# Attention states, soft mixture and gated MLP in one kernel: the products with the states of the middle chunk are moved to the other two quarters of the array and next to a state link of the following iteration

## The chip, the cores and the metric

The kernel runs on one core of a Trainium2 chip. The metric is the device time of one execution in microseconds (us), as the median of the runs. Differences of under 0.5% (2 us) cannot be told from no change here.

## The reference

Everything is float32. A gated linear attention comes first, then a soft mixture of experts over all its tokens, then a gated MLP.

```python
# B, H, S, D = 4, 8, 768, 48
for t in range(S):
    state = alpha[:, :, t, :, None] * state + k[:, :, t] (x) v[:, :, t]    # D x D per head
    y[:, :, t] = q[:, :, t] @ state
x = y as 3072 tokens x 384
logits = x @ phi                         # 32 slots
d = softmax of logits over the tokens;  slot_input = d.T @ x
slot_out[e] = relu(slot_input[e] @ w1[e]) @ w2[e]      # 8 experts, 384 -> 1024 -> 384
x = softmax(logits over the slots) @ slot_out
out = (silu(x @ w_gate) * (x @ w_val)) @ w_out         # 384 -> 1536 -> 384
```

The last three weights come as 64-bit floats. The kernel loads them as pairs of 32-bit words and turns them into float32 itself.

## The kernel before

**Stages.** The attention takes the first 158 us. Then come the experts (first layer at L853, second at L910, until 193 us), and then the MLP with its output until the end. The MLP works with weights and activations split into two rounded parts (L1006, L1007, L1045).

**The attention.** A unit is one batch with two heads, so there are 16 units. The two heads lie on partitions 0 to 47 and 64 to 111. A unit has six chunks of 128 tokens and is worked in two halves of three chunks, so the loop of `fast()` has 32 iterations `g`, with `h = g % 2` the half. An iteration mixes steps of three halves, and the order of each engine's queue is the order in which the code is written (the schedule is manual). In the order of the queues, iteration `g` does this:

- `scan_w(g + 3)`, `scan_p(g + 3)` on DVE: running products of alpha (L307, L314), with small operations between (L306, L309, L310); `scale(g + 2)` on POOL (L325) multiplies q and k with them.
- `emit_st(g, 1 - h)`, the first link of the state chain: two small matmuls add the last state (L402), and ACT scales the sum and writes it to SBUF (L404).
- `emit_s(g + 1)`: the scores of the next half, six matmuls in pairs of 64 rows (L353), head 0 into one PSUM bank and head 1 into another (the tiles `s`).
- `emit_st(g, 2 - h)`, the second link; `emit_kt(g + 1)`, transposes of k (L371, copied by ACT at L374); `emit_xt(g - 1)`, transposes of the output (L462, L466); `emit_masks(g + 1)`: DVE masks the scores of head 0 into SBUF (L360), ACT copies those of head 1 (L362) and POOL masks them (L363); `emit_l(g - 1)`, the logits (L453).
- at the end of every fourth unit, steps of the mixture (`slot_steps`: `peak`, `exps`, `keep`, `e_tok`, `part`, `l_tok`, `c_norm`), one or a few to an iteration.
- `emit_past(g)`: the products of q with the states, two heads x three chunks (L420, the first chunk of a unit has none); `emit_dh(g + 1)`: what the chunks add to the state (L390); `emit_ip(g)`: the products of the masked scores with v, added to the same PSUM tile `y` (L432), which ACT copies whole into the tile `xt` (L434).

**The conversion.** Each of the 24 pieces of the gate and value weights is turned into float32 by four steps: `conv_y` on ACT (L249, writes a buffer `y` in the tile `near`), and `conv(0)`, `conv(1)`, `conv(2)` on DVE (L253, L257, L261); `conv(1)` and `conv(2)` read what `conv_y` wrote. Before, `conv_y` stands at the end of an iteration and the other three in the next one. They run in iterations 2 to 10, 13 to 18, 21 to 26 and 29 to 31.

**Loads.** SP issues all of them in the order of the code. `pump_units` loads the halves' inputs into buffers as these come free, `pump_gv` the weights to be converted, and `pump` the weights of the experts (`w1`, `w2`, 768 KB each) and of the output (`wo`), paced by a credit of `RATE` words an iteration. The last four `w2` go where `w1` blocks of the last group lay, so they wait for that group's matmuls (L853).

Of the kernel before, what the change touches and what calls it, by code (L numbers as in the profile page):

```python
# [33 lines left out]
LAST = 4  # L34
GV0, RATE = 1, 840
TINY = 2.0 ** -55
NEAR, ROUND = 31600, 19184
LA = 3
# [54 lines left out]
def attention_slots_mlp(ctx: ExitStack, tc: tile.TileContext, kq, at, vt, phi, w1, w2, wgv, wo, cst, out):  # L93
# [12 lines left out]
    negm = cs[:, 288:289]  # L106
    phs = const.tile([112, NU, NSL], F32, name="phs")
    tots = const.tile([112, B * NU, NC], F32, name="tots")
# [32 lines left out]
    def program(general):  # L141
# [15 lines left out]

        zn = {nm: [0] * n for nm, n in (("a", 4), ("p", 5), ("v", 4), ("w", 2), ("x", 2))}
        zsize = {"a": HW, "p": HB, "v": 288, "w": HW, "x": 384}
        for z in "a0 a1 p2 a2 p3 v0 w0 a3 p4 v1 w1 p0 v2 p1 v3 x0 x1".split():  # L160
            zn[z[0]][int(z[1])] = ar.alloc(zsize[z[0]], 1)
# [107 lines left out]
        NG = 24  # L269
        gvb, gvy, gvd = {}, {}, [0]  # L270

# [3 lines left out]
        def conv_y():  # L275
            i = gvd[0]
            if i < NG and ("wgv", divmod(i, 4)) in have:
                gvy[i] = to_f32_y(view(have["wgv", divmod(i, 4)]))

        def conv(part):  # L280
            i = gvd[0]
            if i not in gvy:
                return
            n, p = divmod(i, 4)
            raw = view(have["wgv", (n, p)])
            if n not in gvb:
                gvb[n] = need(BLK)
            dst = view((gvb[n][0] + GP * p, GP))
            if part == 0:
                to_f32_z(dst, raw)  # L290
            elif part == 1:
                to_f32_p(dst, gvy[i])
            else:
                to_f32_s(dst, gvy.pop(i))
                gvd[0] += 1
                r = have.pop(("wgv", (n, p)))
                z_g.append(r[0])
# [47 lines left out]
        def emit_s(g, c):  # L345
            n, h = sgs[g]
            k, q = view(kp[g]), view(qp[g])
            if c == 0:
                sps[g] = [pss(), pss()]
            t0 = c * CH  # L350
            o = c * CH
            for s in range(2):
                nc.tensor.matmul(sps[g][s][:, o:o + CH], lhsT=k[64 * s:64 * s + 64, t0:t0 + CH], rhs=q[64 * s:64 * s + 64, t0:t0 + CH], start=True, stop=True)  # L353
# [53 lines left out]

        yps = {}


        def emit_past(g):
            n, h = sgs[g]
            q = view(qp[g], 112)
            yps[g] = ps_y.tile([128, 512], F32, tag="y", name="y")
            for c in range(3):
                cc = 3 * h + c
                o = slice(c * CH, (c + 1) * CH)
                for s in range(2) if cc else ():
                    p = slice(0, 64) if s == 0 else slice(64, 112)
                    nc.tensor.matmul(yps[g][p, o], lhsT=gst[n, cc][p, 0:p.stop - p.start], rhs=q[p, o], start=(cc == max(1, 3 * h)), stop=False, skip_group_check=True)  # L420
            del qp[g]
            release(pair.pop(g), z_p, g + 5)

        def emit_ip(g):
            n, h = sgs[g]
            v = view(vv[g]).rearrange("p (c e) -> p c e", e=96)
            ps = yps[g]
            for c in range(3):
                o = slice(c * CH, (c + 1) * CH)
                for s in range(2):  # L430
                    p = slice(0, 64) if s == 0 else slice(64, 112)
                    nc.tensor.matmul(ps[p, o], lhsT=v[:, c, 48 * s:48 * s + p.stop - p.start], rhs=smk[g, s][:, c], start=False, stop=True, skip_group_check=True)  # L432
            xt[g] = (z_x.pop(0), 384)
            nc.scalar.copy(view(xt[g], 112), ps[0:112, 0:384])  # L434
            del smk[g, 0], smk[g, 1], yps[g]
            release(vv.pop(g), z_v, g + 4)

# [7 lines left out]
        def emit_l(g):  # L445
            n, h = sgs[g]
            b, u = units[n]
            if u == 0 and h == 0:
                lps[b] = ps_l.tile([128, 512], F32, tag="l", name="l")
            x = view(xt[g], 112)  # L450
            for j in range(3):
                t0 = j * CH
                nc.tensor.matmul(lps[b][32 * j:32 * j + 32, CH * h:CH * h + CH], lhsT=phs[:, u, :], rhs=x[:, t0:t0 + CH], start=(u == 0 and h == 0), stop=(u == NU - 1), skip_group_check=True)  # L453

# [13 lines left out]
        def slot_steps(b):  # L468
# [27 lines left out]
            def e_tok():  # L496
# [4 lines left out]
                nc.vector.tensor_copy(st["et"].rearrange("p r e -> p (r e)"), ps[:, 0:192])  # L501

            def part(between=lambda: None):
                ps = psm()
                o = NU * b % 5
                pieces = [(0, o, min(NU, 5 - o))] + [(5 - o, 0, NU - 5 + o)] * (o > 1)
                for r in range(2):
                    if r:
                        between()
                    for u, p, w in pieces:  # L510
                        for j in range(3):
                            nc.tensor.matmul(ps[32 * j:32 * j + 32, 96 * u:96 * u + 96 * w], lhsT=st["et"][:, r, 32 * j:32 * j + 32], rhs=xtok[:, p:p + w, 3 * r + j, :], start=(r == 0 and u == 0), stop=(r == 1), skip_group_check=True)
                if own:
# [62 lines left out]

        def fast():
            pump_units(4)

# [42 lines left out]
            for g in range(NSG):  # L622
                n, h = sgs[g]
                nxt = g + 1 < NSG
                if g + 3 < NSG:
                    scan_w(g + 3, lambda: conv(0))
# [22 lines left out]
                if g:  # L649
                    emit_l(g - 1)  # L650
                    release(xt.pop(g - 1), z_x, g + 1)
                    p = sgs[g - 1][0]
# [35 lines left out]
        def slow():  # L688
# [60 lines left out]
            while gvd[0] < NG:  # L749
                pump_gv()  # L750
                conv_y()
                for i in range(3):
# [376 lines left out]
def _arrays(q, k, v, alpha, moe_phi, moe_w1, moe_w2, moe2_w_gate, moe2_w_val, moe2_w_out):  # L1129
# [16 lines left out]
    vt = c(v.reshape(B, NU, 2, NC, CH, D).transpose(0, 1, 4, 3, 2, 5)).reshape(B, NU, CH, NC * 96)  # L1146
    ph = np.zeros((112, NU, NSL), np.float32)
    pr = moe_phi.reshape(NU, 2, D, NSL)
    for s in range(2):
        ph[64 * s:64 * s + 48] = pr[:, s].transpose(1, 0, 2)  # L1150
    w1 = c(moe_w1.reshape(NE, 3, 128, 2, 512).transpose(0, 3, 2, 1, 4)).reshape(NE, 2, 128, BLK)
# [30 lines left out]
```

## Time and profile before

| | |
|---|---|
| median of three runs | 394.04 us (393.09 to 395.3) |
| profiled execution | 395.87 us, its span 394.1 us |
| granted TensorE clock | 0.986 |
| PE busy | 372.6 us (95% of the span) |
| DVE busy | 291.0 us (74%) |
| ACT busy | 201.5 us (51%) |
| POOL busy | 103.9 us (26%) |

Busy shares are averages over stages with different limits. In the rows of the profile PE is TensorE's matmuls, PEld its weight loads, DVE VectorE, ACT ScalarE, POOL GpSimd and SP the queue that issues loads. Each float32 matmul shows as two records, so six matmuls stand as x12. A matmul's record is longer than the time in which it holds the array: records overlap, and the starts tell how fast they follow each other.

### The profile page before, as it was taken

What the parts mean: (1) busy time and instruction counts of PE and PEld (TensorE: products, weight loads), DVE (VectorE), ACT (ScalarE), POOL (GpSimd) and SP (SyncE); (2) the same over time, 40 slices, a digit from 0 to 9 for tenths busy, and PEclk for the clock granted to TensorE, in tenths of its full rate; (3) what the DMA queues carried; (4) which work ended last, traced back from release to release, by engine and by line L of the source; (5) the groups of instructions that cost most, each with busy time, mean ns of one, the idle gap of its engine ahead of it and who ended that gap; (6) DMA issues with size and microseconds to landing.
All of it is one profiled execution on the core that took longest, in us unless ns stands there. A gap on an engine that the chain in (4) does not pass through costs nothing.

```text
span 394.1 us, 8610 instructions
## 1 busy us (share of the span) xinstructions
PE 372.6 (95%) x3309; PEld 278.1 (71%) x3309; DVE 291.0 (74%) x566; ACT 201.5 (51%) x468; POOL 103.9 (26%) x105
## 2 busy tenths in 40 slices
PE   6999999998998998999799999999999999999992
PEld 3677767776776776434358868888888888888781
DVE  6999997997999773214598995767767877877550
ACT  1456665656466455423267655446445445446431
POOL 3378675788588741020300000000000000000000
PEclk8999999999999999999899999999999999999997
DMA  8899997999799849799900004104114114112002
GB/s 277 316 320 360 351 360 276 312 346 321 258 362 351 289 157 350 288 335 407 400 33 0 1 2 150 39 34 150 35 37 151 37 35 148 39 35 81 2 1 89
DMA packets 28627, 74.25 MB, mean 188 GB/s; under 512 B 3216, under 2 KB 11648, under 8 KB 28576
## 3 DMA queue, kind: packets, MB, share of 16 engines
q1 hardware_dynamic: 28256, 73.27, 52.3%
q8 instruction: 28, 0.46, 0.5%
q10 hardware_dynamic: 272, 0.21, 0.2%
q14 instruction: 23, 0.19, 0.1%
q0 software_dynamic: 48, 0.13, 0.1%
HBM read 68.87 MB, written 4.72 MB: 187 GB/s over the span
## 4 chain that ended last, share of the span: by engine, by line
PE 55%; DVE 6%; DMA 3%; ACT 3%; issue 2%; SPq 0%; DVEq 0%; ACTq 0%
PE m L1045 21%; PE acc L1045 11%; PE s L1006 4%; PE s L1007 4%; DMA near<-w 3%; PE s L853 3%; PE y L432 2%; PE y L420 2%; DVE near L1012 1%; DVE rnd L1020 1%; ACT near L249 1%; PE sw L975 1%; PE l L453 1%; PE m L402 1%; PE m L390 1%
## 5 line engine op out<-in xcount | busy, mean ns | idle before, releaser
L1045 PE MATMUL m<-rnd 128*128 128x512 f32 x432 | 129.2, 389 | 0.0
L1045 PEld LDWEIGHTS m<-rnd 128*128 128x128 f32 x432 | 81.1, 188 | 16.8
L1009 ACT ACTIVATE near<-s 128x512 f32<-128x512 f32 x72 | 43.1, 599 | 79.0 <-PE s L1006 77.3
L1045 PE MATMUL acc<-rnd 128*128 128x512 f32 x216 | 81.1, 392 | 0.8 <-DVE rnd L901 0.8
L325 POOL TENSOR_TENSOR far<-far 112x384 f32<-112x384 f32 x61 | 78.5, 1306 | 6.5 <-DVE tots L309 3.6
L1012 DVE TENSOR_TENSOR near<-near,s 128x512 f32<-128x512 f32 x72 | 49.4, 686 | 36.1 <-ACT near L1009 35.9
L1020 DVE TENSOR_TENSOR rnd<-near,rnd 128x512 fp32r<-128x512 f32 x72 | 49.4, 686 | 3.2 <-ACT rnd L1018 3.1
L1045 PEld LDWEIGHTS acc<-rnd 128*128 128x128 f32 x216 | 40.5, 188 | 10.3 <-DVE rnd L901 1.6
L1018 ACT CAST rnd<-near 128x512 fp32r<-128x512 f32 x72 | 44.3, 615 | 0.2 <-DVE near L1012 0.2
L404 ACT ACTIVATE far<-m,tots 112x48 f32<-112x48 f32 x80 | 24.1, 301 | 29.1 <-PE m L402 17.3
L307 DVE TENSOR_TENSOR_SCAN far<-far,r 112x388 f32<-112x388 f32 x32 | 30.8, 962 | 5.2 <-DMA far<-at 2.5
L353 PE MATMUL s<-far 64*128 64x128 f32 x384 | 30.6, 292 | 2.5 <-DVE r L306 2.1
L1116 DVE TENSOR_REDUCE amm<-near 112x1 f32<-112x768 f32 x32 | 30.3, 947 | 2.5 <-DMA near<-at 2.5
L363 POOL TENSOR_SCALAR_AFFINE_SELECT far<-far 128x384 f32<-128x384 f32 x32 | 19.1, 596 | 48.8 <-ACT far L362 48.8
L314 DVE TENSOR_TENSOR_SCAN far<-far,r 112x387 f32<-112x387 f32 x32 | 30.7, 959 | 1.1
L257 DVE SCALAR_TENSOR_TENSOR near<-near 128x384 uint32<-128x384 uint32 x36 | 24.2, 672 | 7.9 <-ACT near L249 7.0
L434 ACT COPY far<-y 112x384 f32<-112x384 f32 x32 | 15.3, 480 | 28.1 <-PE y L432 28.1
L432 PE MATMUL y<-far 128*48 128x128 f32 (+1 forms) x384 | 28.6, 274 | 0.0
L1006 PE MATMUL s<-rnd 128*128 128x512 f32 x72 | 28.3, 393 | 0.0
L1007 PE MATMUL s<-rnd 128*128 128x512 f32 x72 | 28.1, 391 | 0.0
L353 PEld LDWEIGHTS s<-far 64*128 64x128 f32 x384 | 24.4, 189 | 4.7 <-POOL far L325 2.6
L402 PE MATMUL m<-far,cs 64*64 64x48 f32 (+1 forms) x256 | 19.9, 229 | 6.5 <-ACT far L404 3.8
(163 smaller groups left out, 495.0 us busy)
## 6 DMA issues: line engine op xcount, KB each, us to landing
near<-w SPq DMA_DIRECT2D x18, 768.0 KB, 6.8
far<-kq SPq DMA_DIRECT2D x32, 384.0 KB, 4.8
far<-w SPq DMA_DIRECT2D x14, 768.0 KB, 6.7
near<-wgv SPq DMA_DIRECT2D x24, 384.0 KB, 5.4
far<-at SPq DMA_DIRECT2D x32, 194.0 KB, 4.7
near<-at SPq DMA_DIRECT2D x16, 339.1 KB, 3.3
far<-vt SPq DMA_DIRECT2D x32, 144.0 KB, 4.0
near<-wo SPq DMA_DIRECT2D x12, 384.0 KB, 8.7
```

The costliest lines, as they stand in the source:

```text
L307: nc.vector.tensor_tensor_scan(w[:, ::-1], a[:, ::-1], rst[:, ::-1], 0.0, ALU.mult, ALU.add)
L314: nc.vector.tensor_tensor_scan(a, a, rst[:, 0:387], 0.0, ALU.mult, ALU.add)
L325: eng.tensor_tensor(out=xv, in0=xv, in1=sv, op=ALU.mult)
L353: nc.tensor.matmul(sps[g][s][:, o:o + CH], lhsT=k[64 * s:64 * s + 64, t0:t0 + CH], rhs=q[64 * s:64 * s + 64, t0:t0 + CH], start=True, stop ...
L432: nc.tensor.matmul(ps[p, o], lhsT=v[:, c, 48 * s:48 * s + p.stop - p.start], rhs=smk[g, s][:, c], start=False, stop=True, skip_group_check ...
L1006: nc.tensor.matmul(pg, lhsT=swk[n][:, 128 * o:128 * o + 128], rhs=ctT[t % 4], start=True, stop=True)
L1007: nc.tensor.matmul(pv, lhsT=swk[n][:, 256 + 128 * o:256 + 128 * o + 128], rhs=ctT[t % 4], start=True, stop=True)
L1009: nc.scalar.activation(sg, pg, AF.Silu)
L1012: nc.vector.tensor_tensor(out=h_, in0=sg, in1=pv, op=ALU.mult)
L1018: nc.scalar.copy(hi, h_)
L1020: nc.vector.tensor_tensor(out=lo, in0=h_, in1=hi, op=ALU.subtract)
L1045: nc.tensor.matmul(p, lhsT=passes[j][0][:, sl], rhs=passes[j][1], start=(f == 0 and j == 0), stop=(f == NF - 1 and j == 2))
```

## The change

Five things are changed at once.

1. The middle chunk's products (`emit_past` and `emit_ip`, c = 1) write the other head's half of the output partitions (`swap`), so head 0's products with a state use rows 0 to 63 and columns 64 to 111 of the array and head 1's use rows 64 to 111 and columns 0 to 63. They no longer lie in the tile `y`, but in columns 384 to 511 of the bank that holds head 0's scores. The two score banks are now the same two tiles throughout (`sbank`). ACT copies the output in two instructions. The logits' weights `phi` and the pooled products (`x_rows`) undo the swap.
2. `emit_ip(g)` comes first and opens the accumulation; `emit_past(g)` and the copies follow in iteration `g + 1`, right behind the first state link and ahead of the scores.
3. `conv_y` and `conv(1)` stand behind `emit_kt`, in the same iteration as `conv(0)` and `conv(2)`. They run in iterations 1 to 10, 13 to 18, 21 to 26, 29 and 30.
4. When no inputs of halves are left to load, `pump` is no longer paced.
5. `xt` has one buffer in place of two, `phs` is doubled.

```diff
+        def swap(c):
+            return int(c == 1 and not general)
+        def y_out(g, s, c):
+            p = half(s ^ swap(c))
+            return sbank[0][p, 384:512] if c == 1 else yps[g][p, c * CH:(c + 1) * CH]
+        def emit_ip(g):
+            yps[g] = ps_y.tile([128, 512], F32, tag="y", name="y")
...
+                    o = y_out(g, s, c)
+                    e = 96 * c + 48 * s
+                    nc.tensor.matmul(o, lhsT=v[:, e:e + o.shape[0]], rhs=smk[g, s][:, c], start=(c < 2), stop=True, skip_group_check=True)
...
         def emit_past(g):
...
+                    o = y_out(g, s, c)
+                    nc.tensor.matmul(o, lhsT=gst[n, cc][half(s), 0:o.shape[0]], rhs=q[half(s), c * CH:(c + 1) * CH], start=False, stop=True, skip_group_check=True)
+            xt[g] = (z_x.pop(0), 384)
+            x = view(xt[g], 112)
+            nc.scalar.copy(x[:, CH:2 * CH], sbank[0][0:112, 384:512])
+            x, y = (r.rearrange("p (c t) -> p c t", t=CH)[:, 0::2] for r in (x, yps.pop(g)[0:112, 0:384]))
+            nc.scalar.copy(x, y)
...
+                now[0] = (0 < g <= 8 or g % 8 not in (3, 4)) and gvd[0] < NG and ("wgv", divmod(gvd[0], 4)) in have
+                emit_st(g, 1 - h)
+                if g:
+                    emit_past(g - 1)
...
-                conv(1)
-
-                emit_st(g, 1 - h)
                 if nxt:
                     for c in range(3):
                         emit_s(g + 1, c)
                 emit_st(g, 2 - h)
                 if nxt:
                     emit_kt(g + 1)
+                conv_y()
+                conv(1)
                 if g:
                     emit_xt(g - 1)
...
-                emit_past(g)
...
-                if GV0 <= g and (g < 8 or g % 8 not in (2, 3)):
-                    conv_y()
...
-                credit[0] = min(credit[0] + RATE, 2 * BLK)
+                credit[0] = min(credit[0] + RATE, 2 * BLK) if uloads else NEAR
...
+            emit_past(NSG - 1)
```

In the rows below, `s` are the score banks, `y` the output tile, `m` the PSUM tiles for small products, and `far` and `near` the two SBUF areas. What an instruction waits for stands in brackets, by the engine or DMA queue.

PE, in the products of an iteration's masked scores with v, before:

```order
L432 MATMUL y<-far 64x128
L432 MATMUL y<-far 48x128 [waits Pool_49]
L432 MATMUL y<-far 64x128
L432 MATMUL y<-far 48x128
L432 MATMUL y<-far 64x128
L432 MATMUL y<-far 48x128
```

and now:

```order
L429 MATMUL y<-far 64x128
L429 MATMUL y<-far 48x128 [waits Pool_49]
L429 MATMUL s<-far 48x128 [waits DVE_49]
L429 MATMUL s<-far 64x128
L429 MATMUL y<-far 64x128
L429 MATMUL y<-far 48x128
```

The middle pair writes the score bank. Its wait is for the DVE instruction L359 that masks the next half's scores out of that bank, in the same iteration.

PE, from the first state link to the second, before:

```order
L402 MATMUL m<-far,cs 64x48 [waits Activation_49]
L402 MATMUL m<-far,cs 48x48
L353 MATMUL s<-far 128x128 [waits DMAHW7_49,DVE_49,Pool_49]
L353 MATMUL s<-far 128x128 x5
L402 MATMUL m<-far,cs 64x48 [waits Activation_49]
```

and now:

```order
L401 MATMUL m<-far,cs 64x48 [waits Activation_49]
L401 MATMUL m<-far,cs 48x48
L440 MATMUL y<-far 64x128
L440 MATMUL y<-far 48x128
L440 MATMUL s<-far 48x128
L440 MATMUL s<-far 64x128
L440 MATMUL y<-far 64x128
L440 MATMUL y<-far 48x128
L352 MATMUL s<-far 128x128 [waits DMAHW7_49,Activation_49,Pool_49]
L352 MATMUL s<-far 128x128 x5
L401 MATMUL m<-far,cs 64x48
```

The products with the states now stand between the link and the scores, and the scores' wait for ACT is for the copy L443, which takes those products out of the score bank just ahead of them.

ACT, one iteration with a conversion, before:

```order
L434 COPY far<-y 112x384 [waits PE_49]
L249 ACTIVATE near<-near 128x384 [waits DMAHW7_49,DVE_49,Activation_49]
L404 ACTIVATE far<-m,tots 112x48 [waits PE_49] x2
L374 COPY far<-m 128x224 [waits PE_49,Activation_49]
L466 COPY far<-m 128x288 [waits PE_49]
L362 COPY far<-s 128x384 [waits Pool_49]
```

and now:

```order
L443 COPY far<-s 112x128 [waits DVE_49,PE_49,Activation_49]
L445 COPY far<-y 112x2x128 [waits PE_49,Activation_49]
L403 ACTIVATE far<-m,tots 112x48 [waits PE_49]
L373 COPY far<-m 128x336 [waits PE_49,Activation_49]
L249 ACTIVATE near<-near 128x384 [waits DMAHW4_49,DVE_49,Activation_49]
L477 COPY far<-m 128x288 [waits PE_49]
L361 COPY far<-s 128x384 [waits Pool_49]
```

The conversion's step L249 moved from ahead of the two links to behind the copy of the transposed k. On DVE the order of the operations is the same as before: L257, which reads what L249 writes, stands ahead of the mask.

More of the change, by code (lines that the diff above doesn't have):

```diff
@@ L34 @@
 LAST = 4
-GV0, RATE = 1, 840
+RATE = 840
 TINY = 2.0 ** -55
-NEAR, ROUND = 31600, 19184
+NEAR, ROUND = 31600, 19056
 LA = 3
@@ L269, in program @@
         NG = 24
-        gvb, gvy, gvd = {}, {}, [0]
+        gvb, gvy, gvd, now = {}, {}, [0], [False]
         def gv_part(n, k):
@@ L276, in conv_y @@
             i = gvd[0]
-            if i < NG and ("wgv", divmod(i, 4)) in have:
+            if now[0]:
                 gvy[i] = to_f32_y(view(have["wgv", divmod(i, 4)]))
@@ L281, in conv @@
             i = gvd[0]
-            if i not in gvy:
+            if not now[0]:
                 return
@@ L347, in emit_s @@
             k, q = view(kp[g]), view(qp[g])
[L348 to L349 removed]
+            sps[g] = sbank
             t0 = c * CH
@@ L406, in emit_st, with half @@
                 del dps[g]
-        yps = {}
+        yps, sbank = {}, []
+        def swap(c):
+            return int(c == 1 and not general)
+        def half(s):
+            return slice(0, 64) if s == 0 else slice(64, 112)
+        def y_out(g, s, c):
[3 more added lines that the diff above has]
+            yps[g] = ps_y.tile([128, 512], F32, tag="y", name="y")
+            v = view(vv[g])
+            for c in range(3):
+                for s in range(2):
+                    o = y_out(g, s, c)
+                    e = 96 * c + 48 * s
+                    nc.tensor.matmul(o, lhsT=v[:, e:e + o.shape[0]], rhs=smk[g, s][:, c], start=(c < 2), stop=True, skip_group_check=True)
+            del smk[g, 0], smk[g, 1]
+            release(vv.pop(g), z_v, g + 4)
         def emit_past(g):
@@ L452, in emit_l @@
                 t0 = j * CH
-                nc.tensor.matmul(lps[b][32 * j:32 * j + 32, CH * h:CH * h + CH], lhsT=phs[:, u, :], rhs=x[:, t0:t0 + CH], start=(u == 0 and h == 0), stop=(u == NU - 1), skip_group_check=True)
+                nc.tensor.matmul(lps[b][32 * j:32 * j + 32, CH * h:CH * h + CH], lhsT=phs[:, swap(j), u, :], rhs=x[:, t0:t0 + CH], start=(u == 0 and h == 0), stop=(u == NU - 1), skip_group_check=True)
         def emit_xt(g, between=lambda: None):
@@ L501, in e_tok, with x_rows @@
                 nc.vector.tensor_copy(st["et"].rearrange("p r e -> p (r e)"), ps[:, 0:192])
+            def x_rows(p, w, r, j):
+                x = xtok[:, p:p + w, 3 * r + j, :]
+                if swap(j):
+                    x = bass.AP(x.tensor, x.offset + 48, [list(x.ap[0]), list(x.ap[1]), [-48, 2], [1, 48]])
+                return x
             def part(between=lambda: None):
@@ L511, in part @@
                         for j in range(3):
-                            nc.tensor.matmul(ps[32 * j:32 * j + 32, 96 * u:96 * u + 96 * w], lhsT=st["et"][:, r, 32 * j:32 * j + 32], rhs=xtok[:, p:p + w, 3 * r + j, :], start=(r == 0 and u == 0), stop=(r == 1), skip_group_check=True)
+                            nc.tensor.matmul(ps[32 * j:32 * j + 32, 96 * u:96 * u + 96 * w], lhsT=st["et"][:, r, 32 * j:32 * j + 32], rhs=x_rows(p, w, r, j), start=(r == 0 and u == 0), stop=(r == 1), skip_group_check=True)
                 if own:
@@ L577, in fast @@
         def fast():
+            sbank.extend(pss() for _ in range(2))
             pump_units(4)
@@ L750, in slow @@
                 pump_gv()
+                now[0] = True
                 conv_y()
@@ L1146, in _arrays @@
     vt = c(v.reshape(B, NU, 2, NC, CH, D).transpose(0, 1, 4, 3, 2, 5)).reshape(B, NU, CH, NC * 96)
-    ph = np.zeros((112, NU, NSL), np.float32)
+    ph = np.zeros((112, 2, NU, NSL), np.float32)
     pr = moe_phi.reshape(NU, 2, D, NSL)
     for s in range(2):
-        ph[64 * s:64 * s + 48] = pr[:, s].transpose(1, 0, 2)
+        for x in range(2):
+            ph[64 * s:64 * s + 48, x] = pr[:, s ^ x].transpose(1, 0, 2)
     w1 = c(moe_w1.reshape(NE, 3, 128, 2, 512).transpose(0, 3, 2, 1, 4)).reshape(NE, 2, 128, BLK)
```

25 lines of the change are left out of this document (4 added, 21 removed).

## The prediction

> **What bounds the kernel now.** I read the page first, then the busy time by stretch of the span, then one iteration of the attention engine by engine, the waits, and the end of the experts.
>
> ```profile
> PE 372.6 (95%) x3309; PEld 278.1 (71%) x3309; DVE 291.0 (74%) x566; ACT 201.5 (51%) x468; POOL 103.9 (26%) x105
> ...
> DVE  6999997997999773214598995767767877877550
> ```
>
> PE is busy almost throughout. DVE's slices show nines in the attention (the first 16 of 40), so there a second engine is nearly full. The stretches below are cut at first links; after the stretch come its length and the busy time of PE, PEld, DVE, ACT and POOL, the granted clock, the DMA share and GB/s.
>
> ```profile
> 12.82:16.12 3.30, 3.30 (x52) 2.58 (x51) 3.06 (x7) 1.33 (x4) 0.65 (x2) 1.00 0.93 364
> 16.12:51.29 35.17, 33.90 (x511) 26.07 (x509) 33.67 (x74) 20.88 (x59) 23.91 (x25) 1.00 0.95 329
> 51.29:70.94 19.65, 18.69 (x273) 13.85 (x271) 16.44 (x38) 11.35 (x34) 12.44 (x13) 1.00 0.90 316
> 70.94:88.36 17.42, 16.90 (x256) 12.97 (x254) 16.72 (x39) 10.65 (x30) 13.76 (x13) 1.00 0.94 330
> ...
> 108.21:125.64 17.43, 16.91 (x257) 12.98 (x255) 16.73 (x39) 10.66 (x30) 13.78 (x13) 1.00 0.98 358
> ...
> 145.48:154.18 8.70, 8.45 (x130) 6.49 (x128) 3.75 (x8) 5.31 (x15) 2.51 (x4) 1.00 0.77 289
> ...
> 180.00:200.00 20.00, 17.52 (x175) 7.52 (x167) 12.72 (x25) 7.18 (x15) 3.53 (x3) 0.91 0.92 364
> ```
>
> The first row is iteration 0, the second iterations 1 to 8, then 9 to 12, 13 to 16, 21 to 24, and 29 and 30. In 1 to 8, 13 to 16 and 21 to 24 PE is 96 or 97% busy and DVE 96%: a wait on a chain over PE, ACT and DVE has no slack to hide in. Iterations 1 to 8, 13 to 16, 21 to 24, 29 and 30 are the 18 with a conversion and no large step of the mixture; they take 35.17 + 17.42 + 17.43 + 8.70 = 78.72 us, 4.37 each.
>
> Iteration 5, from one first link to the next, on PE, ACT and DVE:
>
> ```profile
> 33.55 0.38 PE L432 MATMUL y<-far 128*64 128x128 f32 x3
> 33.86 0.31 PE L402 MATMUL m<-far,cs 64*64 64x48 f32 x4
> 34.10 0.94 PE L353 MATMUL s<-far 64*128 64x128 f32 x12
> 35.17 0.31 PE L402 MATMUL m<-far,cs 64*64 64x48 f32 x4
> 35.41 0.51 PE L371 MATMUL m<-cs,far 112*128 112x112 f32 x3
> ...
> 36.48 0.86 PE L420 MATMUL y<-far 64*64 64x128 f32 x12
> 37.28 0.49 PE L390 MATMUL m<-far 128*64 128x48 f32 x11
> 37.59 0.28 PE L432 MATMUL y<-far 128*48 128x128 f32 x1
> ...
> 38.43 0.31 PE L402 MATMUL m<-far,cs 64*64 64x48 f32 x4
> ```
>
> ```profile
> 34.36 0.57 ACT L249 ACTIVATE near<-near 128x384 f32<-128x384 f32 x1
> ...
> 35.53 0.30 ACT L404 ACTIVATE far<-m,tots 112x48 f32<-112x48 f32 x1 [0.42 <-PE m L402]
> 36.01 0.44 ACT L374 COPY far<-m 128x336 f32<-128x336 f32 x1 [0.17 <-PE m L371]
> 36.35 0.40 ACT L466 COPY far<-m 128x288 f32<-128x288 f32 x1
> ```
>
> ```profile
> 35.44 0.53 DVE L257 SCALAR_TENSOR_TENSOR near<-near 128x384 uint32<-128x384 uint32 x1
> 35.89 0.55 DVE L360 TENSOR_TENSOR far<-s,cs 128x384 f32<-128x384 f32 x1
> ```
>
> The conversion's ACT step (L249) runs 0.50 us after the first link, so L257 never waits for it, and the mask (L360) is done at 36.44, 1.15 us before the products of the masked scores start (37.59).
>
> **The change part by part.** *New chain in the conversion iterations.* By the order of the instructions, the middle pair of those products now waits for the mask of the same iteration, since both touch head 0's score bank. On DVE the mask still stands behind L257, L257 reads what L249 writes, and L249 now stands on ACT behind the copy of the transposed k, which waits for the transposes behind the second link. So a ring closes within one iteration. I add it up from the first link at T.
>
> From T to the scores: the link holds PE for 0.24 us (33.86 to 34.10). L420's three chunks take 0.80 us (36.48 to 37.28), 0.27 a chunk. If the middle chunk runs beside the first in the other two quarters, it is issued by T + 0.51. The copy L443 starts 0.12 later, as L404 does (35.53, where the link's 0.24 ended at 35.41), and takes what the smallest copy of 128 columns takes:
>
> ```profile
> L515 ACT COPY pall<-m x2: 262/316/370, 60.8 to 61.0; 96x128 f32<-96x128 f32 x1, 96x256 f32<-96x256 f32 x1
> ```
>
> 0.26, with 0.05 for PE to go on (my allowance): the scores start at S = T + 0.94. Bounds: T + 0.77 if the copy is never waited for (the two diagonal chunks alone), T + 1.20 if the middle chunk runs beside nothing. No row of before has four quarters at work. I take the lower case for the products, since L420's two heads already share a chunk's time.
>
> [...]
>
> From S on, with the scores' own time read where nothing holds the second link:
>
> ```profile
> 62.55 0.94 PE L353 MATMUL s<-far 64*128 64x128 f32 x12
> 63.42 0.31 PE L402 MATMUL m<-far,cs 64*64 64x48 f32 x4
> ```
>
> scores 0.87; second link 0.24; transposes to their copy's start 0.60 (35.41 to 36.01); copy to L249's start 0.34 (36.01 to 36.35); L249 0.57 and 0.03 to start L257; L257 0.45 until the mask starts (35.44 to 35.89); mask 0.55 and 0.05 for PE. That is 3.70, so the middle pair starts at S + 3.70. Without that wait it would follow the other steps: the first pair of these products stands 37.59 − 34.10 = 3.49 us behind the scores here, and the middle comes four records of 0.07 later, 0.28; less L420's 0.80, which have moved, and less the 0.20 that the second link stood late (35.17 − 34.10 = 1.07 against 0.87), it is S + 2.77. PE waits about a microsecond, with L432's remaining pairs and everything of the next iteration behind it.
>
> Eight of the 12 records remain: the last three stand 0.31 ahead of the next link (33.55 to 33.86), the other five 0.07 each (37.59 to 38.43 for 12): 0.66. The iteration is 0.94 + 3.70 + 0.66 = 5.30. With h = 0 two chunks of k are transposed:
>
> ```profile
> 31.27 0.41 PE L371 MATMUL m<-cs,far 112*128 112x112 f32 x2
> ```
>
> 0.10 less in the transposes (0.41 against 0.51) and about 0.10 less in the copy: 5.10. Mean 5.20; 18 × 5.20 = 93.6 against 78.72: **+14.9 us**. DVE (33.67 us in eight iterations, 4.21 each) is no longer near full, so the rest of its work hides in the wait, and POOL (23.91) too. Bounds: S at T + 0.77 gives +11.8, at T + 1.20 +19.6; and L257 has a longer form, as the seven from 22.2 to 48.5 show (min, median, max):
>
> ```profile
> L257 DVE SCALAR_TENSOR_TENSOR near<-near x7: 530/902/908, 22.2 to 48.5; 128x384 uint32<-128x384 uint32 x7
> ```
>
> 0.37 more in every iteration would be +6.7. I take the short form, the one in the iteration that I add up; the long one is priced as a rival.
>
> *Iterations without a conversion* (9 to 12 and the like, 19.65 us for four): the mask follows the scores directly,
>
> ```profile
> 63.52 0.56 DVE L360 TENSOR_TENSOR far<-s,cs 128x384 f32<-128x384 f32 x1 [0.84 <-PE s L353]
> ```
>
> and ends 1.53 us after their start, so the second wait costs nothing. PE gives L420's 0.80 and spends 0.70 between link and scores. I take 0 for these twelve, ends −3 and +3 (a quarter of a microsecond each way, the doubt about S).
>
> *Iteration 0*: DVE's mask stands late there.
>
> ```profile
> 16.14 0.53 DVE L360 TENSOR_TENSOR far<-s,cs 128x384 f32<-128x384 f32 x1
> ```
>
> It ends at 16.67; with 0.05 and 0.66 the next link comes at 17.4 in place of 16.12: **+1.3**. *Iteration 31*: its second link waits, and the moved products fill about half of it.
>
> ```profile
> 155.46 0.31 PE L402 MATMUL m<-far,cs 64*64 64x48 f32 x4 [0.98 <-ACT far L404]
> ```
>
> **−0.5**, ends 0 and −1.
>
> *Loads unpaced.* One `w2` more leaves before the experts, so the four that wait for the last group arrive earlier.
>
> ```profile
> 186.15 1.47 PE L910 MATMUL so<-near 128*32 128x384 f32 x16
> 187.99 0.85 PE L910 MATMUL so<-near 128*32 128x384 f32 x8 [0.36 <-DMA near<-w]
> 189.90 0.85 PE L910 MATMUL so<-near 128*32 128x384 f32 x8 [1.05 <-DMA near<-w]
> 191.81 1.51 PE L910 MATMUL so<-near 128*32 128x384 f32 x8 [1.06 <-DMA near<-w]
> 193.25 1.11 PE L774 MATMUL m<-cs,near 128*128 128x128 f32 x4
> ```
>
> ```profile
> 186.98 1.89 DVE L943 TENSOR_SCALAR rnd<-near 128x256 fp32r<-128x256 f32 x4
> ...
> 190.29 1.78 DVE L770 COPY near<-ct 128x512 f32<-128x512 f32 x3
> ```
>
> Waits of 0.36 + 1.05 + 1.06 = 2.47 go. L774 then waits for the first of DVE's three copies L770, 190.29 + 0.6 = 190.9, in place of 193.25: **−2.3**, ends 0 and −2.5. [...]
>
> Sum: 14.9 + 0 + 1.3 − 0.5 − 2.3 = +13.4. The profiled execution (span 394.1, time 395.87) would become 409.3. The median is 394.04, 1.8 lower, and the difference is put on that: **407.4 us**.
>
> **The rivals.** *Faster, about 385.* The waits are hidden: this happens if the mask ends 1 us earlier than I add up, by S + 2.7. Then 1 to 8 shrink to PE's and DVE's own busy time (33.9, 33.67), 13 to 16 and 21 to 24 to 16.9, 29 and 30 by the wait for the second link, in all −1.3 − 1.0 − 0.7 = −3; the others −3 and the experts −2.3. For it: 74% DVE on average. Against it: the order of L249 on ACT.
>
> *Same, about 394.* The ring is longer than before by only 0.13 us an iteration, 18 × 0.13 = 2.3, what the experts give back. That needs L249 to start 0.7 earlier, ahead of the copy of k.
>
> *Slower still, about 415.* The quarters don't run side by side (+4.7) and L257 stays long in half of the iterations (+3.4): 415.5. For it: the 0.91 row. PE's clock may also fall where it idles: 0.91 in 180 to 200, where it waits for loads, though 1.00 in all stretches of the attention.
>
> *The shared bank costs nothing*: the middle pair and the mask use different columns of the bank. The order shows the wait all the same, so this would be the first rival. [...]
>
> **How the numbers follow.** Forecast (400 to 412) 0.74, slower still 0.13, faster 0.08, same 0.05. With all terms at their lower ends the change is 11.8 − 3 + 1.3 − 1 − 2.5 = +6.6, or 400.6; I set the low end of the range halfway from there to the rival of no change, at 397, and the high one at 416, which takes in the slower rival. A difference of under 0.5% (2 us) cannot be told from none. Faster 0.08, same 0.05, slower 0.87.
>
> **What would show it.** Of the changed kernel: conversion iterations of 5.1 to 5.3 us with a wait on PE of about 1 us in the middle pair of L429 for DVE's L359; L257 waiting for ACT's L249 in each; L249 2 us later than the scores' start; L352 waiting 0.1 to 0.4 for L443; iterations 9 to 12 still 19.6 in all; no wait for `w` at L910 above 0.4. I am wrong if L249 starts less than 1.1 us behind the scores, or if L429 shows no wait.

## The result: 22.7 us slower, and the profile after

The changed kernel takes 417.38 us in the median of four runs (415.81 to 418.4), against 394.67 for the kernel before beside it: ratio 1.0562 (95% interval 1.0513 to 1.061). Medians here and below are of all runs, a few slow ones included (one of 401.89 us among those of the kernel before, which is 394.04 without it), and ratios are of the runs without them. The forecast was 407.4, the range 397 to 416: the time lies above the range; the sign and the main term were right, the size too small. The profiled execution has a span of 416.7 us, 22.6 more than before.

The page, its lines for busy time and for the granted clock in 40 slices:

```profile
PE 373.9 (90%) x3308; PEld 275.0 (66%) x3309; DVE 293.1 (70%) x566; ACT 203.6 (49%) x500; POOL 92.9 (22%) x105
...
PEclk9779999999699969999999999999999999999997
```

Before, the clock's line had a first 8 and then nines to the end of the attention. Now it has sevens in two early slices, and a six near 105 and one near 150 us. The busy time by stretch, cut at first links as before (iteration 1; 2 to 8; 9 to 12; 13 to 16; 17; 18 to 20; 21 to 24; 25; 26 to 28; 29 and 30; 31 to its last masked product):

```profile
18.07:25.14 7.07, 6.86 (x66) 5.09 (x65) 3.56 (x10) 2.98 (x9) 1.46 (x2) 0.50 0.74 231
25.14:61.88 36.74, 29.42 (x446) 21.25 (x445) 29.31 (x63) 19.28 (x60) 18.68 (x22) 0.98 0.86 288
61.88:81.72 19.84, 17.75 (x273) 12.79 (x271) 17.10 (x40) 11.28 (x38) 9.84 (x12) 1.00 0.90 298
81.72:102.75 21.03, 16.44 (x256) 11.85 (x254) 16.11 (x36) 10.97 (x34) 12.75 (x14) 1.00 0.85 277
102.75:110.89 8.14, 6.65 (x69) 4.90 (x67) 6.04 (x14) 3.78 (x13) 3.71 (x5) 0.65 0.78 269
110.89:126.11 15.22, 13.90 (x218) 10.34 (x217) 12.18 (x30) 7.60 (x24) 6.92 (x8) 0.96 0.74 227
126.11:146.85 20.74, 16.43 (x256) 11.85 (x254) 16.10 (x36) 10.84 (x34) 12.74 (x14) 1.00 0.94 317
146.85:154.75 7.90, 6.40 (x69) 4.67 (x67) 6.04 (x14) 3.78 (x13) 3.71 (x5) 0.67 0.63 206
154.75:170.11 15.36, 14.05 (x218) 10.63 (x217) 12.09 (x29) 7.62 (x24) 6.91 (x8) 0.95 0.81 262
170.11:180.50 10.39, 8.23 (x130) 5.93 (x128) 3.54 (x7) 5.44 (x17) 3.00 (x5) 1.00 0.63 232
180.50:183.30 2.80, 2.51 (x43) 1.63 (x44) 0.00 (x0) 1.42 (x5) 0.00 (x0) 1.00 0.44 134
```

Two things are to be seen. Where the clock is 1.00, PE's busy share fell from 97% to 78% (16.44 of 21.03). And iterations 1, 17 and 25 run at clocks of 0.50 to 0.67, where PE is busy for longer than the same work took before (6.65 us in iteration 17, against 4.76). Term by term, after less before:

| | before | after | change | forecast |
|---|---|---|---|---|
| end of iteration 0 | 16.12 | 18.07 | +1.95 | +1.3 |
| the 18 conversion iterations | 78.72 | 43.81 + 21.03 + 20.74 + 10.39 = 95.97 | +17.25 | +14.9 |
| 9 to 12 | 19.65 | 19.84 | +0.2 | 0 |
| 17 to 20, 25 to 28 | 19.85 + 19.84 | 23.36 + 23.26 | +6.9 | 0 |
| iteration 31 | 3.98 | 2.80 | −1.2 | −0.5 |
| from there to the end (rest of the 22.6) | | | −2.5 | −2.3 |

Iteration 4, an undisturbed conversion iteration, on PE, ACT and DVE:

```profile
35.95 0.25 PE L401 MATMUL m<-far,cs 64*64 64x48 f32 x2
35.98 0.33 PE L440 MATMUL s<-far 64*48 64x128 f32 x2
...
36.99 0.94 PE L352 MATMUL s<-far 64*128 64x128 f32 x12 [0.28 <-POOL far L325]
...
38.10 0.41 PE L370 MATMUL m<-cs,far 112*128 112x112 f32 x2
...
39.30 0.44 PE L429 MATMUL y<-far 128*48 128x128 f32 x4
40.52 0.44 PE L429 MATMUL s<-far 128*48 128x128 f32 x4 [0.78 <-DVE far L359]
40.78 0.40 PE L429 MATMUL y<-far 128*48 128x128 f32 x4
41.11 0.25 PE L401 MATMUL m<-far,cs 64*64 64x48 f32 x2
```

```profile
36.63 0.27 ACT L443 COPY far<-s 112x128 f32<-112x128 f32 x1
...
38.61 0.34 ACT L373 COPY far<-m 128x224 f32<-128x224 f32 x1
38.85 0.56 ACT L249 ACTIVATE near<-near 128x384 f32<-128x384 f32 x1
```

```profile
39.46 0.54 DVE L257 SCALAR_TENSOR_TENSOR near<-near 128x384 uint32<-128x384 uint32 x1
39.92 0.55 DVE L359 TENSOR_TENSOR far<-s,cs 128x384 f32<-128x384 f32 x1
```

The ring stands there link by link: copy of k 38.61, L249 38.85, L257 39.46, mask 39.92 to 40.47, middle pair 40.52. The scores' wait is put down to POOL's L325, but they start 0.09 us after the copy L443 ends (36.90), and again at 42.03 after 41.94: it is the copy they wait for.

What the forecast priced at nothing is a pause of PE followed by a slow clock. In iteration 0 the mask stands behind DVE's scans; in iterations 17 and 25 the mixture's exponentials (L499 to L505) stand on ACT ahead of L443:

```profile
17.02 0.69 PE L429 MATMUL s<-far 128*48 128x128 f32 x4 [2.87 <-DVE far L359]
```

```profile
103.34 0.47 ACT L499 ACTIVATE e<-l,nmx 96x256 f32<-96x256 f32 x1 [1.62 <-PE y L440]
...
103.99 0.35 ACT L505 COPY lt<-l 96x256 f32<-96x256 f32 x1
104.24 0.30 ACT L403 ACTIVATE far<-m,tots 112x48 f32<-112x48 f32 x1
104.44 0.26 ACT L443 COPY far<-s 112x128 f32<-112x128 f32 x1
```

```profile
104.79 1.27 PE L352 MATMUL s<-far 64*128 64x128 f32 x12 [1.49 <-POOL far L325]
```

The scores' record grew from 0.94 to 1.27 us, and L429's records behind the pause of 2.87 us from 0.44 to 0.69. The granted clock was 0.50 from 16.49 to 26.73, from 105.24 to 112.06 and from 149.61 to 156.44 us, and 1.00 in the rest of the attention from 11 us on.

### The profile page after: what moved, and what is told of

Read it like the earlier page. It is cut to its first block, busy times and chain, and to the rows that moved or that the text cites. A ratio compares the mean times of both kernels' runs of the same rounds, so it can differ in the third digit from the quotient of the medians.

```text
span 416.7 us, 8741 instructions
## 1 busy us (share of the span) xinstructions
PE 373.9 (90%) x3308; PEld 275.0 (66%) x3309; DVE 293.1 (70%) x566; ACT 203.6 (49%) x500; POOL 92.9 (22%) x105
## 4 chain that ended last, share of the span: by engine, by line
PE 62%; issue 10%; DVE 8%; POOL 6%; DMA 5%; ACT 3%; SPq 0%; ACTq 0%; POOLq 0%; DVEq 0%
PE m L1067 21%; PE acc L1067 11%; POOL far L325 6%; DMA far<-kq 4%; PE s L1028 4%; PE s L352 4%; PE s L1029 4%; PE s L875 3%; PE so L932 2%; PE m L401 2%; PE m L370 2%; DMA far<-at 2%; PE y L440 2%; PE y L429 2%; PE s L429 1%
## 5 line engine op out<-in xcount | busy, mean ns | idle before, releaser
L325 POOL TENSOR_TENSOR far<-far 112x384 f32<-112x384 f32 x61 | 69.7, 1160 | 8.9 <-DVE far L307 4.4
L403 ACT ACTIVATE far<-m,tots 112x48 f32<-112x48 f32 x80 | 24.2, 302 | 73.3 <-PE m L401 70.6
L257 DVE SCALAR_TENSOR_TENSOR near<-near 128x384 uint32<-128x384 uint32 x36 | 20.0, 557 | 33.8 <-ACT near L249 32.8
L352 PEld LDWEIGHTS s<-far 64*128 64x128 f32 x384 | 25.9, 194 | 20.9 <-POOL far L325 17.1
L362 POOL TENSOR_SCALAR_AFFINE_SELECT far<-far 128x384 f32<-128x384 f32 x32 | 16.7, 522 | 84.0 <-ACT far L361 84.0
L429 PE MATMUL y<-far 128*48 128x128 f32 (+1 forms) x256 | 30.1, 291 | 0.0
L429 PE MATMUL s<-far 128*48 128x128 f32 (+1 forms) x128 | 15.3, 305 | 16.1 <-DVE far L359 16.1
L261 DVE SCALAR_TENSOR_TENSOR near<-near 128x384 uint32<-128x384 uint32 x36 | 22.8, 632 | 0.3
```

The lines of the kernel that those rows point to most:

```text
L325: eng.tensor_tensor(out=xv, in0=xv, in1=sv, op=ALU.mult)
L429: nc.tensor.matmul(o, lhsT=v[:, e:e + o.shape[0]], rhs=smk[g, s][:, c], start=(c < 2), stop=True, skip_group_check=True)
```

## The experiments

Each kernel ran beside the kernel before on the same chip. A ratio is to that kernel; the changed kernel's is 1.0562.

| kernel | median us | ratio (95% interval) |
|---|---|---|
| mask first | 404.71 | 1.0207 (1.0133 to 1.0282) |
| conversion early | 399.8 | 1.0104 (1.0067 to 1.0141) |
| exponentials later | 412.14 | 1.0454 (1.0385 to 1.0523) |
| filled pause | 414.59 | 1.0494 (1.0415 to 1.0573) |
| iteration 0 | 415.09 | 1.0501 (1.0447 to 1.0556) |
| one bank, no quarters | 395.13 | 0.999 (0.9948 to 1.0033) |
| loads alone | 395.04 | 0.9975 (0.994 to 1.001) |
| conversion as before | 395.79 | 0.9995 (0.9957 to 1.0033) |
| three put right | 391.6 | 0.9916 (0.988 to 0.9953) |
| the same, no quarters | 394.16 | 0.9995 (0.9963 to 1.0028) |
| the same, no bank, no quarters | 386.36 | 0.9788 (0.9753 to 0.9822) |
| three put right, products first | 388.53 | 0.9864 (0.981 to 0.9917) |

**Mask first.** DVE's mask ahead of L257.

```diff
...
                 conv_y()
+                if nxt:
+                    emit_masks(g + 1, (0,))
                 conv(1)
...
-                    emit_masks(g + 1)
+                    emit_masks(g + 1, (1,))
```

> The changed kernel, with DVE's mask of head 0 placed ahead of the conversion's step L257 in DVE's queue. Ring theory (the conversion iterations are long because the middle pair waits for a mask that stands behind L257, L249 and the copy of the transposed k): the mask ends about 1.5 us after the scores' start, PE's wait of 0.75 us in each of the 18 iterations goes, 13 to 14 us less than the changed kernel, about 403.5; what is left over the kernel before is the clock's halves (iterations 0 to 2, 17, 25) and the copy's wait. Rival (the moved products, the copy and the four quarters cost the time themselves): within 3 us of the changed kernel, 414 to 420.

The ratio fell by 0.0355, 14 us: the ring theory's size. From iteration 13 on the conversion iterations last 4.12 to 4.46 us and L429 waits for no mask (iteration 15 alone takes 4.63, with a longer wait at the scores). In iterations 3 to 8 a wait for the mask remained, 0.39 to 1.36 us. Behind the longest of these, in iteration 8, the scores of iteration 9 waited 1.62 us and the clock was 0.50 from 60.48 to 67.31: in the profiled execution iterations 8 and 9 took 3.9 us more than in the changed kernel, so in that execution the ring alone gave more. The pauses in 17 and 25 were still there (1.55 and 1.58 us), and the mean clock of that execution was 0.971, against 0.966 in the changed kernel's.

**Conversion early.** L249 ahead of the copy of k, DVE's order untouched.

```diff
                 if g:
                     emit_past(g - 1)
+                conv_y()
...
-                conv_y()
                 conv(1)
```

> The changed kernel, with the conversion's ACT step ahead of the links' scaling of the second link and of the copy of the transposed k (behind the output's copies); DVE's order untouched. Ring theory: L249 starts about 2 us earlier, L257 no longer waits for it, the mask ends before the middle pair wants it: 13 to 14 us less than the changed kernel, about 403.5, as in the run with the mask first. Rival one (only the mask's place on DVE matters, L249's not): no more than 3 us less. Rival two (L249 in the way of the second link's scaling on ACT costs what it gives): 408 to 412.

0.0458, 18 us: more than expected. Moving either link of the ring undoes it, which shows that it is this chain and neither step alone. Iterations 17, 18, 25 and 26 are 6.6 us shorter besides: the maximum that the exponentials need stands behind the mask on DVE, the pauses there are 1.12 and 0.74 us in place of 1.5, and the clock is 1.00 from 94 to 106 us, with iteration 17 in it; its mean is 0.982, against 0.966. In iterations 3 to 8 the middle pair still waits and takes part of that back. One of DVE's rows of that kernel:

```profile
50.34 0.36 DVE L253 TENSOR_SCALAR near<-near 128x384 uint32<-128x384 uint32 x1 [1.01 <-DMA near<-wgv]
```

The first conversion step, ahead of the mask in the queue, waits for its piece of the weights to arrive. With all four steps in one iteration the piece is wanted an iteration earlier; this cost lay hidden under the ring.

**Exponentials later**, and **filled pause**. The first moves the exponentials behind the copies. The second keeps the wait and gives PE seven matmuls to do in it.

```diff
# exponentials later
                 if g:
                     emit_past(g - 1)
+                if late:
+                    pend.pop(0)()
+                    pend.pop(0)()
...
-                if late:
-                    pend.pop(0)()
-                    pend.pop(0)()
# filled pause
+                if late and g > 9:
+                    keep_warm(7, psm())
                 if nxt:
                     for c in range(3):
                         emit_s(g + 1, c)
```

> The changed kernel, with the mixture's exponentials and the copy of the logits (ACT) moved behind the output's copies in the next iteration. Clock theory (a pause of PE of 1.5 us in iterations 17 and 25 halves its clock for the 7 us that follow): the scores wait under 0.5 us there, the granted clock stays at 1.00 from 100 to 160 us, and iterations 17 to 19 and 25 to 27 are 3 to 4 us shorter each: 6 to 7 us less, about 410.5. Rival (only the pause itself costs): 1 us less for each, 415.

> The changed kernel, with seven idle-work matmuls (128x512, bf16, into a free PSUM tile) ahead of the scores in iterations 17 and 25, which fill the pause of 1.5 us and remove no wait. Clock theory: the clock stays at 1.00 there, and the two places are 2 to 3 us shorter each though the wait remains: 4 to 6 us less than the changed kernel, about 412.5. Rival (the slow stretch behind the pause isn't the pause's doing): 0 to 1 us more, 417 to 418.5.

Iteration 17 in the stretches of the two kernels, exponentials later and then filled pause:

```profile
101.30:106.52 5.22, 4.41 (x68) 3.16 (x66) 5.05 (x12) 3.68 (x13) 2.70 (x4) 1.00 1.00 354
```

```profile
103.22:109.61 6.39, 5.96 (x75) 3.74 (x73) 5.11 (x12) 3.67 (x13) 2.69 (x4) 1.00 0.83 302
```

Against 8.14 at a clock of 0.65, the filled pause gives 1.75 us with the wait still there, and 0.36 more in iteration 18: the slow stretch is the pause's doing, about 2.1 us a pause, and the pause itself costs another 1.17 (6.39 against 5.22). In all the filled pause took 0.0068 off the ratio, 2.7 us, where 4 to 6 were expected, though the two places alone give 4.1. Exponentials later: 0.0108, 4.3 us, where 6 to 7 were expected. The places gave 6.4 us by iterations, and iteration 9 lost 0.55. The intervals of both overlap that of the changed kernel, so the reading rests on the iterations.

**Iteration 0.** The scans behind the mask, in iteration 0 alone.

```diff
-                if g + 3 < NSG:
+                if not g:
+                    pass
+                elif g + 3 < NSG:
                     scan_w(g + 3, lambda: conv(0))
...
                     emit_masks(g + 1)
+                    if not g:
+                        scan_w(3)
+                        scan_p(3)
```

> The changed kernel, with DVE's two scans of iteration 0 moved behind its mask, so that the mask follows the scores. Clock theory (PE's pause of 2.87 us in iteration 0 halves the clock until 26 us): the mask ends near 14.5 us, the pause shrinks to about 0.5, iterations 1 and 2 run at a clock of 1.00 and iteration 3 starts near 26.5 in place of 30.7: 4 us less than the changed kernel, about 413. Rival (DVE's scans, not the mask, hold iterations 0 and 1 anyway): under 1 us.

In the profile as expected: iterations 0 to 2 at a clock of 1.00, and iteration 3 starts at 26.50 in place of 30.73. The median fell by 2.4 us only (0.0061), of 4, and the intervals overlap. Its rows also say more of what the clock does: iterations 0 to 2, then 17 and 25 with their scores' waits.

```profile
12.76:26.50 13.74, 11.02 (x171) 8.12 (x170) 12.10 (x27) 6.78 (x21) 6.01 (x9) 1.00 0.85 296
98.52:104.87 6.35, 4.42 (x69) 3.17 (x67) 5.13 (x12) 3.68 (x13) 2.70 (x4) 1.00 0.90 304
...
140.50:148.23 7.73, 6.23 (x68) 4.59 (x66) 6.04 (x14) 3.79 (x13) 3.71 (x5) 0.70 0.65 212
```

```profile
100.57 0.94 PE L352 MATMUL s<-far 64*128 64x128 f32 x12 [1.50 <-POOL far L325]
```

```profile
142.55 0.94 PE L352 MATMUL s<-far 64*128 64x128 f32 x12 [1.50 <-POOL far L325]
```

The same pause of 1.50 us left the clock alone the first time and cut it to 0.70 the second. The runs of a kernel spread by up to 6 us, those of the kernel before nearly as far (392.82 to 398.41), and the longer ones mostly have the lower mean clock: here 411.85 us at 0.987, 414.32 at 0.973, 415.86 at 0.972 and 417.85 at 0.962. So single terms of 2 to 4 us are read here from iterations and not from medians.

**One bank, no quarters**, and **conversion as before**. The first takes the score bank and the swap away and leaves the order; the second leaves bank and quarters and puts the conversion back.

```diff
# one bank, no quarters (with one copy again, and the accumulation opened at c == 0 alone)
-            return int(c == 1 and not general)
+            return 0
...
-            return sbank[0][p, 384:512] if c == 1 else yps[g][p, c * CH:(c + 1) * CH]
+            return yps[g][p, c * CH:(c + 1) * CH]
...
# conversion as before: conv(1) ahead of the scores, L249 at the end of the iteration
+                conv(1)
                 if nxt:
                     for c in range(3):
                         emit_s(g + 1, c)
...
-                conv_y()
-                conv(1)
...
+                if 1 <= g and (g < 8 or g % 8 not in (2, 3)):
+                    conv_y()
...
```

> The changed kernel, with the middle chunk's output back in the tile y and on the diagonal quarters as before the change; the order of the products, of the conversion and of the loads stays as changed. Bank theory (the score bank, not the new order, makes both waits): no wait for the mask at L429 and none for the copy at the scores, the conversion iterations return to 4.2 to 4.4 us, the pauses in iterations 0, 17 and 25 and the clock's halves go too; 394 to 400. Rival (the new place of the products and of L249 costs by itself): above 408.

> The changed kernel, with the conversion's four steps where they were: L249 at the end of an iteration, the other three in the next one. Ring theory: no wait of 0.75 us at L429 in the conversion iterations, which last 4.15 to 4.3 us; and as a piece of the gate and value weights is wanted an iteration later than with L249 early, DVE doesn't wait for its load in iterations 3 to 9. 17 to 19 us less than the changed kernel, 398.5 to 400.5. Rival (in iterations 3 to 9 the ring runs through something else than the load): 401 to 404, with waits at L429 of 0.2 to 0.8 us there.

Iterations 13 to 16 of the two:

```profile
71.88:88.39 16.51, 16.29 (x256) 12.70 (x254) 14.40 (x33) 10.83 (x30) 12.16 (x12) 1.00 0.95 311
```

```profile
75.67:92.85 17.18, 15.57 (x256) 11.94 (x254) 16.25 (x37) 11.01 (x34) 15.25 (x13) 1.00 0.94 327
```

Either edit brings the time back to that of the kernel before. The ring needs both: the shared bank and L249's new place. The first was expected to lose the pauses in iterations 17 and 25 too. The scores' waits went, but the second link waits there 1.16 and 1.21 us for ACT's scaling (L403), and behind the 1.16 the clock was 0.50 from 93.35 to 96.77, so that iteration 18 took 6.29 us. In the second, iterations 3 to 7 last 4.17 to 4.27 us with no wait at L429, so there the rest of the wait was the load's. It beat its expectation by 3 to 5 us, although iterations 0 and 1 are still as slow as in the changed kernel.

**Loads alone**, on the kernel before.

```diff
-                credit[0] = min(credit[0] + RATE, 2 * BLK)
+                credit[0] = min(credit[0] + RATE, 2 * BLK) if uloads else NEAR
```

> The kernel before, with the loads of weights unpaced once the inputs are all issued, and nothing else. Theory: the waits for w2 at the second layer (0.36, 1.05 and 1.06 us) go and the clock's dip behind them too: 2 to 3 us less than the kernel before, ratio 0.993 to 0.995. Rival (the last four w2 wait for the last group and arrive no earlier): within 0.5 us.

```profile
190.74 0.85 PE L910 MATMUL so<-near 128*32 128x384 f32 x8 [0.50 <-DMA near<-w]
192.68 0.85 PE L910 MATMUL so<-near 128*32 128x384 f32 x8 [1.08 <-DMA near<-w]
193.46 0.66 PE L774 MATMUL m<-cs,near 128*128 128x128 f32 x4
```

Inconclusive in the median, 1 us with an interval from −2.4 to +0.4. In this profile the attention ends 1.96 us later than in the profile before and L774 starts 0.21 later, 1.75 us less between the two; the waits fell from 2.47 to 1.58, and did not go. The other 0.86 would fit the clock: before, it was 0.50 from 191.78 to 195.19, behind the waits of 1.05 and 1.06 us, and here the last eight matmuls of L910 took 0.85 us and the first four of L774 0.66, where before they took 1.51 and 1.11.

**Three put right**, and what is left of the change then. The conversion as before, the exponentials later and iteration 0 together; then the same without quarters, without bank and quarters, and with the products ahead of the first link, whose edit is

```diff
...
-            for c in range(3):
+            for c in (1, 0, 2):
...
             nc.scalar.copy(x[:, CH:2 * CH], sbank[0][0:112, 384:512])
+            link()
...
-                emit_st(g, 1 - h)
                 if g:
-                    emit_past(g - 1)
+                    emit_past(g - 1, lambda: emit_st(g, 1 - h))
+                else:
+                    emit_st(g, 1 - h)
```

> The changed kernel with three things put right: the conversion where it was before the change, the exponentials behind the output's copies, the scans of iteration 0 behind its mask. By the runs so far the first gives 21 to 22 us, the third 4 (the clock's halves in iterations 0 to 2), the second 1 to 2 (pauses of 1.14 us in iterations 17 and 25 shrink to 0.38): 389 to 391.5, about 1% under the kernel before. Rival (what the pauses give is lost to the next wait): 394 to 396.

> The kernel with the three things put right, and the middle chunk's products back on the diagonal quarters (no swap), still in the score bank. If four quarters run at once, the middle chunk's products now come behind the first chunk's, 0.22 to 0.27 us later, and the copy and the scores with them: 32 times that, 6 to 8 us more than with the quarters, 396 to 398. If the quarters don't run at once: the same as with them, within 1.5 us.

> The kernel with the three things put right, without the quarters and without the score bank (the middle chunk in the tile y, one copy). What the two together are worth: the scores wait for no copy (0.29 to 0.38 us an iteration), against 0.2 us more of products. Theory (they cancel to within 0.1 us an iteration): within 3 us of the kernel with both. Rival (the quarters are worth more than the copy costs): 4 us or more above it.

> The kernel with the three things put right, and the products with the states ahead of the first link, the middle chunk first; the copy out of the score bank stands ahead of the link's scaling on ACT, the other copy behind it. The link and the other chunks then cover the copy: the scores start 0.8 us after the iteration's last masked product in place of 0.92 to 1.04, 0.15 to 0.25 us less an iteration, 5 to 7 us less than without, 383 to 386. Rival (the second link's wait for ACT takes the place of the copy's): 388 to 390.

Three put right came out at 391.6, 0.1 above its range, and 0.0079 (3.1 us) below the conversion as before alone, where the other two pieces were to give 5 to 6. In the profiles iterations 0 to 2 do give about 5 us. The exponentials give 0.15: 17 and 25 are 0.43 shorter each, but 18 and 26 are 0.21 and 0.50 longer. Iterations 21 to 24 of the first three, in that order:

```profile
106.59:123.48 16.89, 15.56 (x256) 11.94 (x254) 16.27 (x37) 10.82 (x33) 15.61 (x13) 1.00 0.94 329
```

```profile
108.40:125.80 17.40, 16.43 (x256) 12.81 (x254) 16.27 (x37) 11.07 (x33) 15.03 (x13) 1.00 0.99 344
```

```profile
102.78:119.55 16.77, 16.22 (x256) 12.69 (x254) 16.21 (x34) 10.51 (x29) 14.63 (x13) 1.00 0.99 356
```

The quarters are real: with the bank kept they take 0.87 us of PE's busy time out of four iterations (15.56 against 16.43), 0.22 each, and 3.1 us of the whole (0.0079), less than the 6 to 8 expected. Part of it is lost in idle time: PE idles for 1.33 us of the four iterations with the quarters and 0.97 without. But the bank in which they write costs more: without the bank the scores follow the products at once, and the kernel is 8 us faster (0.0207) than with the bank and no quarters, the same but for the bank and its second copy, and 5 us faster (0.0128) than with both. No run has the quarters without the shared bank. Theory (within 3 us) and rival (the quarters worth more) were both wrong on that, and on the side that neither had. PE of the kernel without bank and quarters, one iteration:

```profile
110.85 0.31 PE L401 MATMUL m<-far,cs 64*64 64x48 f32 x4
110.98 0.63 PE L440 MATMUL y<-far 48*48 48x128 f32 x8
111.55 0.94 PE L352 MATMUL s<-far 64*128 64x128 f32 x12
112.42 0.31 PE L401 MATMUL m<-far,cs 64*64 64x48 f32 x4
```

The products follow the link by 0.13 us, where before the next step followed by 0.24. There the next step was the scores, of another shape than the link; that this is the reason is not shown. Iteration 23 takes 4.05 us with PE busy throughout, against 4.58 before. This version, 386.36 us, is faster than both kernels. What of its edits makes it faster than the kernel before (the new order of the products, the loads, the exponentials' and the scans' new places) no run takes apart.

With the products ahead of the link the gain over three put right is 2 us (0.0052, with overlapping intervals), not 5 to 7. In the profiles it is 3.9 us from iteration 1's scores to iteration 30's (129.18 against 133.11), but this execution's first scores in the loop start 1.7 us later. The time fits the rival's 388 to 390; its wait at the second link isn't there. Where three chunks have such products, the scores mostly wait 0.13 us. Where only two have, what is left to run behind the middle one is too short to cover the copy, and the scores wait 0.29 us, or 0.42 where L249, now the copy's neighbour on ACT, stands just ahead of it and itself waits for DVE:

```profile
113.43 0.56 ACT L249 ACTIVATE near<-near 128x384 f32<-128x384 f32 x1 [0.69 <-DVE r L306]
113.89 0.25 ACT L443 COPY far<-s 112x128 f32<-112x128 f32 x1
```

## Why the prediction was right in its main term and 9 us short

The sum, 13.4, falls 9.2 short of the profile's 22.6: 7.1 us lie in the twelve iterations taken at 0, 2.35 in the conversion iterations, 0.65 in iteration 0, and −0.9 in the last two terms. The step that failed most is "I take 0 for these twelve".

- **Ring in the conversion iterations: right, and shown.** Forecast 5.20 us an iteration, measured 5.15 to 5.23 in 15 of the 18. S came at T + 1.04 and T + 0.92 (forecast 0.94), L249 1.86 us after the scores' start ("2 us later"), L257 in its short form (mean 557 ns over all 36), PE's wait 0.73 to 0.78 where the text said about a microsecond. Four kernels, each of which breaks another link of the ring (mask first, conversion early, conversion as before, no bank), gave 14 to 23 us back, the pauses that went with it included.
- **Iteration 0: right wait, wrong price.** The forecast had the mask end at 16.67 and added 1.3 us; it ended at 16.97, and the pause of 2.87 us that it makes was costed at a clock of 1.00. The clock was 0.50 in all of iteration 1: 1.95 us at the end of iteration 0, 0.65 more than forecast, then 1.85 in iteration 1 (7.07 against 5.22) and 0.43 in iteration 2. The step that failed here is this term together with the 18 × 5.20, which took all 18 as undisturbed.
- **"I take 0 for these twelve": wrong, +7.1 us.** The step counted PE's time and the mask's wait, but not what else stands on ACT ahead of the link's scaling and the copy L443. In iterations 17 and 25 that is the exponentials. Of the 5.4 us in 17, 18, 25 and 26 the clock makes about 4.1 and the pause the rest, by the filled pause. About 1.8 more is the copy's wait and the mixture's other steps in 19, 20, 27, 28 and 12.
- **The clock** stood in the prediction as half a sentence of the rival "slower still", with the 0.91 row, and had no price, though that row has one: behind pauses of 1.05 and 1.06 us the clock was 0.50 for 3.41 us. The iterations show about 7 us: up to 2.9 in 0 to 2 and 4.1 in 17, 18, 25 and 26. With it the sum, 13.4, becomes 20.4 of the 22.6.
- **Quarters side by side: right.** They take 0.22 us of PE's time out of an iteration where the bank is kept. The scores wait for the copy behind them 0.28 and 0.38 us, within the 0.1 to 0.4 forecast.
- **Last loads −2.3, iteration 31 −0.5**: −2.5 and −1.2. One wait at L932 remained, 0.57 us, so the waits give 1.9; the rest would fit the half clock that stands behind them before and not here. Size and place agree in part by luck: with the same loads, waits of 1.14 and 1.06 us were left in the kernel without quarters.
- **The rivals.** Faster and same needed L249 0.7 to 1 us earlier, and did not come; in the kernel with the conversion early, where that is done, the middle pair's wait left iterations 13 to 30. *Slower still* came near its number (415.5) by neither of its two prices: the quarters ran side by side and L257 stayed short. *The shared bank costs nothing* did not come: PE waits for the mask of that bank in 17 of the 18 conversion iterations.

## What to carry to other kernels

The product put into a free corner of a shared PSUM bank took on that bank's readers here: it waited 0.73 to 0.78 us an iteration for the mask in the other columns, and the next scores waited 0.28 and 0.38 us for its copy. Write down for each reader what stands ahead of it on its own engine, because a small conversion step two links up the chain set the period here. When a wait is added, look for the iteration in which something else stands in that queue (the first one, and the one with the rare steps): the mean iteration was forecast within 0.02 us, and the rare ones made most of the miss. Price a pause of TensorE with the slow stretch that may stand behind it, about 2 us here for a pause of 1.5.

## What the runs showed of the hardware

In the traces of the two kernels the granted clock is 1.00 or 0.50. In the attention of the changed kernel it was 0.50 for 10.24 us behind a pause of PE of 2.87 us, all 7.07 us of iteration 1 among them, and for 6.82 and 6.83 us behind pauses of 1.49 and 1.50 us. In the kernel before it was 0.50 for 3.41 us behind 1.05 and 1.06 us, and with the exponentials later it was 0.50 from 19 to 21 us, behind pauses of 0.49 and 1.05 us within three microseconds. In the kernel with one bank and no quarters a pause of 1.16 us had 0.50 behind it.

Other pauses had no slow stretch behind them. With pauses of 0.73 to 0.78 us in the iterations 13 to 16 and 21 to 24 of the changed kernel the clock was 1.00 throughout (81.72 to 102.75 and 126.11 to 146.85 us), and with one of 1.12 us (conversion early) it was 1.00 from 94 to 106 us. The kernel with iteration 0 put right has both cases of one length: behind its first pause of 1.50 us the clock was 1.00 until 110.33 us and three transposes of k (L370) took 0.51 us; behind the second the mean was 0.70 from 140.50 to 148.23 us, and three took 0.82. So the length of a pause alone does not tell whether the clock falls, and no run here takes apart what else decides it.

With seven matmuls in the gap (filled pause) the clock was 1.00 in the 6.39 us of both iterations, 17 and 25.
